# A fused attention and long-convolution kernel: ScalarE instead of GpSimd issues half of four output stores at the end

## The chip, the core and the metric

The kernel runs on one core of a Trainium2 chip. The core has a matrix engine (TensorE, PE in the profile), a vector engine (VectorE, DVE), an engine for activations and copies (ScalarE, ACT), a general engine (GpSimd, POOL) and one that only issues transfers and waits (SyncE, SP). Sixteen DMA engines move data between the core's memory and DRAM; SP, ACT and POOL can issue transfers to them, each through its own queue. Each engine works through its own list of instructions in order. The metric is the device time of one execution in microseconds (us).

## The reference, cut to what matters

Eight batches of 3136 rows. For each batch:

```
scores = z @ z.T / 3136                 # 3136 x 3136, z has 64 columns
attn   = max(scores, 0) ** 2
x      = u * (attn @ v)                 # 3136 x 256
x1, x2, x3 = split(x @ w_proj)          # 3 parts of 256 columns
conv   = irfft(rfft(x2, axis=rows) * rfft(filter, axis=rows))
out    = (x1 * conv * x3) @ w_out       # 3136 x 256, float32
```

The output of one batch is 3136 x 256 numbers of four bytes, 3.2 MB.

## The kernel before, in words

A batch's rows are cut into seven chunks of 512, 512, 512, 512, 512, 256 and 320 columns of the transposed work (`CHUNKS`, line 23), each of two to four tiles of 128 rows. For each chunk the scores are made on TensorE, squared after a relu by ScalarE and VectorE, and multiplied with `v`. The result is multiplied with `u`, projected with `w_proj`, and its middle part goes through a Fourier transform written as matrix products in two stages, with a scratch array in DRAM between the stages. When a batch's spectrum is done, `add_end` (line 1315) finishes it chunk by chunk: it loads the chunk of the convolution (`load_c`), does the last small transform on TensorE (`mm`), multiplies it with the gates on VectorE (`ev`, line 1342), multiplies with `w_out` on TensorE (`mo`), copies the product from the matrix engine's result banks to a tile of the core's memory on ScalarE or VectorE (`eo`, line 1378; such a copy is called an eviction below), and stores the tile (`store`, line 1400).

The order of all instructions is written by a planner when the program is made (`Plan`, line 184). Each piece of work is a `Task` with a cost on one or several engines, the tasks it needs, and the buffers it takes. The planner keeps a clock for each engine, and always emits the task that can start first by those clocks. For ACT, DVE, SP and POOL the method `pick` (line 336) chooses, by the start, then by priority, then by the order in which the tasks were made. A task that moves data has an argument `moves`, and `run` (line 231) adds the delay `DMA_GO` of the issuing engine (line 63), the time on a common bus, and `DMA_DONE`. None of this happens on the chip: there each engine simply runs its list, and waits at semaphores.

The last batch ends differently from the others (line 1865). Its chunks are finished in the order `FINAL`, which is 0, 2, 4, 6, 1, 3, 5, with the flag `split=True`, and their output tiles lie in buffers that are free by then: chunks 0 and 6 in `R_t`, chunks 2, 1 and 5 in `xh`, chunks 4 and 3 in `gs_t`. These names show which chunk a line of the profile belongs to. With `split`, a chunk's tile of 128 partitions is stored in two halves of 64 partitions:

```
elif split:
    s_ = on("POOL", lambda nt=nt, store=store: store(0, nt, (0,), nc.gpsimd), 0.6, [*oe, *behind], moves=0.22 * nt)
    s_ = on("SP", lambda nt=nt, store=store: store(0, nt, (1,)), 0.8, [*oe, *behind], prio=1, moves=0.22 * nt)
```

So POOL issues half 0 of chunks 0, 2, 4, 6, 1 and 3, and SP half 1. Both wait for all evictions of the chunk (`oe`). The last chunk, 5, has a branch of its own (lines 1406 to 1412): one task of SP, in which SP issues half 0 and ACT half 1. A half is 256 KB, that of chunk 6 on POOL 192 KB, and the halves of chunk 5 and the second of chunk 6 are 128 KB.

After the program's last instruction of each engine stands a closing part, which the profile puts down to line 1932: every engine drains, SP waits for the last transfers, and POOL leads a barrier of all engines.

Of the kernel before, what the change touches and what calls it, by code (L numbers as in the profile page):

```python
# [59 lines left out]
    return sum(n / 2400 + 0.003 for n in ns)  # L60


DMA_GO, DMA_DONE = {"SP": 0.3, "POOL": 2.0}, 0.9
LAT = {"PE": 0.22, "ACT": 0.22, "DVE": 0.19, "POOL": 0.15, "SP": 0.0}


# [327 lines left out]
def kernel(  # L394
# [10 lines left out]
    nc = tc.nc  # L405
# [136 lines left out]
    def job(kind, emit, cost, deps=(), takes=(), **kw):  # L542
        if not isinstance(cost, dict):
            cost = {"PE": cost}
        return plan.add(Task(emit, cost, deps, takes, **kw), kind)
# [4 lines left out]
    def on(engine, emit, cost, deps=(), takes=(), **kw):  # L550
        return job(None, lambda e: emit(), {engine: cost}, deps, takes, **kw)
# [18 lines left out]
    def rows_n1(x):  # L570
        return x.rearrange("(n1 n2) d -> n1 n2 d", n2=N2)

    def runs(lo, hi):
        got = []
        for c in range(NC):
            a, b = max(lo, T0[c]), min(hi, T0[c + 1])
            if a < b:
                got.append((0, a, b, NT - T0[c + 1] + a - T0[c]))
        if lo < min(hi, NT - 1):
            got.append((1, lo, min(hi, NT - 1), NT + lo))  # L580
        return got
# [138 lines left out]
    for i, (t0, t1) in enumerate(zip(z_cuts, z_cuts[1:])):  # L720
        step_ = -(-(t1 - t0) // -(-(t1 - t0) // 8))
        for g0 in range(t0, t1, step_):
            nt = min(step_, t1 - g0)
# [375 lines left out]
    for t0 in range(0, NT, 2):  # L1099
        nt = min(2, NT - t0)  # L1100
# [214 lines left out]
    def add_end(b, lasts, gtasks, cs, kind="FB", src=c_p, dsts=(o_p,), late=0, behind=(), then=(), split=False, mids=(y_p,)):  # L1315
        for at, c in enumerate(cs):
            t0, nt = T0[c], len(tiles[c])
# [42 lines left out]
            oe = []  # L1360
# [39 lines left out]
            def store(i0, n, only=(0, 1), by=nc.sync, c=c, ob=ob):  # L1400
                r = rows_n1(out[b])
                for j, lo, hi, n2 in runs(T0[c] + i0, T0[c] + i0 + n):
                    if j in only:
                        by.dma_start(out=r[:, n2 : n2 + hi - lo, :], in_=ob["o"][ds(j * N1, N1), i0 : i0 + hi - lo, :])

            if split and c == cs[-1]:

                def both_queues(nt=nt, store=store):
                    store(0, nt, (0,))
                    store(0, nt, (1,), nc.scalar)  # L1410

                s_ = on("SP", both_queues, 0.6, [*oe, *behind], prio=1, moves=0.45 * nt)
            elif b == B - 2:
                s_ = on(
                    "POOL", lambda nt=nt, store=store: store(0, nt, by=nc.gpsimd), 1.2, [*oe, *behind],
                    moves=0.45 * nt, late=LATE_POOL,
                )
            elif split:
                s_ = on("POOL", lambda nt=nt, store=store: store(0, nt, (0,), nc.gpsimd), 0.6, [*oe, *behind], moves=0.22 * nt)
                s_ = on("SP", lambda nt=nt, store=store: store(0, nt, (1,)), 0.8, [*oe, *behind], prio=1, moves=0.22 * nt)  # L1420
            else:
                s_ = on("SP", lambda nt=nt, store=store: store(0, nt), 1.3, [*oe, *behind], prio=1, moves=0.45 * nt, late=LATE_OUT * (dst is o_p))
# [333 lines left out]
    for gi, g in enumerate(groups):  # L1756
        deps = []
        for un in g:
            b, c, k = un
# [20 lines left out]
        for i, un in enumerate(g):  # L1780
            b, c, k = un
# [46 lines left out]
            if last:  # L1828
# [24 lines left out]
                if c == NC - 1:  # L1853
                    mine = [x for x in x_evs if x[0] == b]
                    gts = [t for x in mine for t in x[2]]
                    lasts = add_spectrum(b, [p for x in mine for p in x[1]])
                    last_spec = loads[-1:]
                    if b < B - 2:
                        add_end(b, lasts, gts, range(NC))
                    elif b == B - 2:  # L1860
                        add_end(b, lasts, gts, range(HOLD))
                        held = lasts, gts
                        held_w = w_
                    else:
                        add_end(b, lasts, gts, FINAL, "FB", A_p, (R_p, xh_p, gs_p, R_p, xh_p, gs_p, xh_p), split=True, mids=(y_p, uT_p))
                        early = [*held[0], held_w]
                        outs = (cut_out, cut_out, cut_out, o_p)
                        add_end(b - 1, early, held[1], range(HOLD, NC), "FZ", cut_in, outs, 4, [(last_spec[0], ISSUED)], [q_])
                        for t in put_back:
                            join(t, inverses[-1], ISSUED)  # L1870
                        late_ones = plan.queues["FZ"]
                        waiting = [t for t in late_ones if t.left and any(d in inverses for d, _ in t.deps)]
                        kids = [k for t in waiting for k in t.kids if k.kind == "FZ"]
                        rest = [t for t in late_ones if t not in waiting and t not in kids]
                        plan.queues["FZ"] = rest + [t for t in late_ones if t in waiting or t in kids]
                    if b == 0:
                        hold = Held(v_p.slots, v_slot[0])
                        w_.frees.append((hold, 0))
                    else:
                        w_.frees.append((cv[b][0], 0))  # L1880
# [56 lines left out]
```

## Time and profile before

| | |
|---|---|
| time, median of 3 runs | 990.45 us (990.18 to 990.82) |
| the profiled execution | 992.91 us, of which the span from first to last instruction is 991.0 us |
| busy over the span | PE 95%, ACT 87%, DVE 84%, POOL 21% |
| granted TensorE clock, mean | 0.989 |
| last instruction that computes | ends at about 979.85 us of the span |
| last issue of a store | starts at 980.83 us of the span |

Times inside the profile are counted from the span's start. A row of the timeline shows the start, the length, the engine, the line of the program, the operation and the tile; a "q" behind the engine (SPq, ACTq, POOLq) marks an instruction of its sequencer: an issue of a transfer, a wait or a drain. The length of an issue is the time for which the issuing engine was held, not that of the transfer. A row of grouped instructions shows the smallest, median and largest length in ns, and the starts of the first and the last. A row of a window shows for a stretch of time the busy time of each engine with the number of instructions, then the granted clock, the busy share of the DMA engines, and what they moved in GB/s. A row of waits shows who waited for whom, with the total, the number and the longest, in us.

### The profile page before, as it was taken

Reading aid. Unit: us, or ns where it says so; the run is one execution under the profiler, and the core shown is the slowest. Engines: PE = TensorE matmul, PEld = TensorE weight load, DVE = VectorE, ACT = ScalarE, POOL = GpSimd, SP = SyncE. Lnnn points to the kernel's source line nnn. Section 1 sums busy time; section 2 is a strip of 40 time slices with the busy share of each in tenths; the row PEclk is TensorE's granted clock in tenths of the full one; section 3 lists DMA queues with packets and bytes.
Section 4 is the critical chain, followed back from the end, with each engine's and each line's share of the span. In section 5 each row is a group of like instructions: output and inputs, shape, how many; then the busy total and the mean of one; then the engine's idle time right before and its main releaser. Section 6 shows DMA issues by size and latency. Waiting matters only on the chain.

```text
span 991.0 us, 19581 instructions
## 1 busy us (share of the span) xinstructions
PE 946.0 (95%) x6774; PEld 471.2 (48%) x6878; DVE 831.3 (84%) x1461; ACT 857.8 (87%) x1192; POOL 207.7 (21%) x430
## 2 busy tenths in 40 slices
PE   6999999999999999999999999999999999999984
PEld 2344544455544545445454444445454455544643
DVE  7966798999798887988789887898879988799874
ACT  5988888899888997899988989799988899998673
POOL 5142311212021312113111320122202230001031
PEclk9999999999999999999999999999999999999978
DMA  9799879979899679997799788997889968985676
GB/s 159 144 174 168 134 151 169 177 131 168 190 206 179 127 150 220 195 174 149 148 219 200 152 137 161 218 200 136 162 171 220 193 126 175 186 219 108 167 214 199
DMA packets 332355, 170.32 MB, mean 172 GB/s; under 512 B 242582, under 2 KB 307926, under 8 KB 332256
## 3 DMA queue, kind: packets, MB, share of 16 engines
q1 hardware_dynamic: 302720, 132.82, 63.3%
q0 software_dynamic: 29456, 36.12, 23.6%
q8 instruction: 54, 0.88, 0.4%
q14 instruction: 45, 0.37, 0.1%
q10 hardware_dynamic: 80, 0.13, 0.0%
HBM read 90.26 MB, written 53.35 MB: 145 GB/s over the span
## 4 chain that ended last, share of the span: by engine, by line
PE 77%; DVE 7%; issue 6%; ACT 4%; DMA 4%; SPq 1%; POOL 1%; POOLq 0%; ACTq 0%; DVEq 0%
PE ps_o_t L523 44%; PE ps_s L523 32%; DVE A_t L1801 4%; ACT R_t L1792 3%; DVE xT_t L1843 1%; DMA uT_t<-un_t 1%; DMA spec<-s_t 1%; DMA ost_t<-in_z_dram 1%; DMA M_t<-spec 1%; ACT s_t L556 1%; SPq L996 0%; DMA specf<-s_t 0%; DVE gs_t L560 0%; ACT gs_t L556 0%; DVE xh L1250 0%
## 5 line engine op out<-in xcount | busy, mean ns | idle before, releaser
L1792 ACT ACTIVATE R_t<-ps_s 128x1024 f32<-128x1024 f32 (+4 forms) x512 | 467.5, 963 | 83.0 <-PE ps_s L523 79.3
L523 PE MATMUL ps_o_t<-A_t,v_t 128*128 128x512 bf16 (+4 forms) x2006 | 447.2, 353 | 11.9 <-issue 5.2
L1801 DVE TENSOR_TENSOR A_t<-R_t 128x1024 bf16<-128x1024 f32 (+2 forms) x324 | 354.1, 1112 | 55.5 <-ACT R_t L1792 55.0
L523 PEld LDWEIGHTS <-v_t 128*128 128x128 bf16 (+1 forms) x2884 | 248.9, 98 | 260.6 <-issue 81.4
L1799 ACT ACTIVATE A_t<-R_t 128x1024 bf16<-128x1024 f32 (+3 forms) x172 | 175.0, 1026 | 1.2
L523 PE MATMUL ps_s<-zT_t 64*64 64x512 bf16 (+4 forms) x1526 | 173.5, 358 | 1.5 <-DVE zT_t L560 0.5
L606 POOL COPY tick<-xT_t 1x1 bf16<-1x1 bf16 x54 | 19.5, 362 | 695.9 <-DVE xT_t L1843 695.9
L523 PE MATMUL ps_s<-xT_t,wp 128*128 128x512 bf16 (+2 forms) x418 | 102.8, 352 | 4.5 <-ACT R_t L1792 2.3
L523 PEld LDWEIGHTS <-zT_t 64*64 64x64 bf16 (+1 forms) x1559 | 52.1, 101 | 107.8 <-issue 93.2
L556 ACT ACTIVATE x_t<-ps_s 128x512 bf16<-128x512 f32 (+2 forms) x170 | 89.7, 583 | 11.8 <-PE ps_s L523 10.1
L1843 DVE SCALAR_TENSOR_TENSOR xT_t<-ps_o_t,uT_t 128x256 bf16<-128x256 f32 (+2 forms) x224 | 76.0, 382 | 8.7 <-PE ps_o_t L523 5.6
L523 PE MATMUL ps_o_t<-M_t,v_t 128*128 128x512 bf16 (+2 forms) x352 | 82.3, 353 | 0.1
L1250 DVE TENSOR_TENSOR xh<-xh,H 128x1024 bf16<-128x1024 bf16 x120 | 82.0, 684 | 0.2
L1162 DVE TENSOR_TENSOR gate_t<-ps_s,x_t 128x256 bf16<-128x256 f32 (+2 forms) x212 | 70.3, 383 | 14.0 <-PE ps_s L523 12.9
L1344 DVE TENSOR_TENSOR yT_t<-ps_s,gate_t 128x512 bf16<-128x512 f32 (+2 forms) x100 | 59.0, 619 | 11.1 <-PE ps_s L523 10.3
L523 PEld LDWEIGHTS <-wp 128*128 128x128 bf16 x448 | 42.9, 98 | 47.1 <-issue 11.0
L597 POOL DMA_DIRECT2D un_t<-in_u_dram x112 | 59.8, 556 | 6.4 <-issue 4.5
L616 POOL DMA_DIRECT2D v_t<-in_v_dram x112 | 59.4, 555 | 3.8 <-PE ps_s L523 1.7
L560 DVE CAST xh<-ps_s 128x512 bf16<-128x512 f32 x61 | 41.1, 688 | 22.6 <-PE ps_s L523 21.3
L523 PE MATMUL ps_s<-wp,xT_t 128*128 128x256 bf16 x396 | 56.3, 273 | 0.1
L523 PE MATMUL ps_s<-wo,yT_t 128*128 128x256 bf16 (+1 forms) x350 | 51.7, 274 | 1.7 <-DVE yT_t L1344 1.7
L556 ACT ACTIVATE s_t<-ps_s 128x512 bf16<-128x512 f32 (+1 forms) x82 | 46.8, 589 | 2.1 <-PE ps_s L523 1.1
(160 smaller groups left out, 828.4 us busy)
## 6 DMA issues: line engine op xcount, KB each, us to landing
out_dram<-ost_t SPq DMA_DIRECT2D x60, 256.0 KB
spec<-s_t SPq DMA_DIRECT2D x96, 128.0 KB
spec_in_t<-spec SPq DMA_DIRECT2D x60, 192.0 KB
spec<-gs_t SPq DMA_DIRECT2D x59, 192.0 KB
v_t<-in_v_dram POOLq DMA_DIRECT2D x80, 128.0 KB, 4.4
un_t<-in_u_dram POOLq DMA_DIRECT2D x80, 128.0 KB, 5.1
conv_in_t<-spec SPq DMA_DIRECT2D x33, 256.0 KB
out_dram<-ost_t SPq DMA_DIRECT2D x18, 128.0 KB
```

The lines of the kernel that those rows point to most:

```text
L523: wrote(nc.tensor.matmul(o, *args, **kw), o)
L556: got = nc.scalar.activation(out_, in_, AF.Copy)
L560: got = nc.vector.tensor_copy(out_, in_)
L597: nc.gpsimd.dma_start(out=t[ds(j * N1, N1), lo - t0 : hi - t0, :], in_=x[:, n2 : n2 + hi - lo, :])
L616: nc.gpsimd.dma_start(out=t[ds(j * N1, N1), ds(v_at(a), (b - a) * D)], in_=r[:, n2 + a - lo : n2 + b - lo, :].rearrange("p t d -> p (t d)"),)
L1162: got = nc.vector.tensor_tensor(g[:, ::-1] if h == 0 else g, p, x, ALU.mult)
L1250: nc.vector.tensor_tensor(x[:, 1 - i], x[:, 0], h, ALU.mult)
L1344: got = nc.vector.tensor_tensor(yb["y"][:, dh, 0:w], p, gates[b, c, dh][:, 0:w], ALU.mult)
L1792: has_read(nc.scalar.activation(blocks(box["R"], n, cw)[:rows], p, AF.Relu), p)
L1799: nc.scalar.activation(a, r, AF.Square)
L1801: nc.vector.tensor_tensor(a, r, r, ALU.mult)
L1843: nc.vector.scalar_tensor_tensor(x, f, inv_s2, ut, ALU.mult, ALU.mult)
```

## The change

For the third to sixth chunk of the last batch's order (4, 6, 1 and 3), half 0 is issued by ACT instead of POOL. Chunks 0 and 2 keep POOL, chunk 5 keeps its branch, and SP's halves stay. The planner is given a delay for transfers that ACT issues, and the cost of such an issue on ACT is put at 0.55 us.

```diff
-DMA_GO, DMA_DONE = {"SP": 0.3, "POOL": 2.0}, 0.9
+DMA_GO, DMA_DONE = {"SP": 0.3, "ACT": 0.5, "POOL": 2.0}, 0.9
...
+            elif split and c in cs[:2]:
+                s_ = on("POOL", lambda nt=nt, store=store: store(0, nt, (0,), nc.gpsimd), 0.6, [*oe, *behind], moves=0.22 * nt)
+                s_ = on("SP", lambda nt=nt, store=store: store(0, nt, (1,)), 0.8, [*oe, *behind], prio=1, moves=0.22 * nt)
             elif split:
-                s_ = on("POOL", lambda nt=nt, store=store: store(0, nt, (0,), nc.gpsimd), 0.6, [*oe, *behind], moves=0.22 * nt)
+                s_ = on("ACT", lambda nt=nt, store=store: store(0, nt, (0,), nc.scalar), 0.55, [*oe, *behind], moves=0.22 * nt)
                 s_ = on("SP", lambda nt=nt, store=store: store(0, nt, (1,)), 0.8, [*oe, *behind], prio=1, moves=0.22 * nt)
```

The store on ACT becomes a task like the evictions: the planner places it in ACT's list between them by its own clocks, at the same priority.

## The prediction

> **What bounds the kernel now.** I began with the page's head and its busy shares.
>
> ```profile
> span 991.0 us, 19581 instructions
> PE 946.0 (95%) x6774; PEld 471.2 (48%) x6878; DVE 831.3 (84%) x1461; ACT 857.8 (87%) x1192; POOL 207.7 (21%) x430
> ```
>
> TensorE bounds the kernel as a whole, and POOL is nearly idle. But these are means over 991 us, and the edit touches only the last 18. So the next view is the busy time of all engines in stretches of that end.
>
> ```profile
> core 0: us, PE busy (x) PEld busy (x) DVE busy (x) ACT busy (x) POOL busy (x), PEclk, DMA share, GB/s
> 974.50:977.00 2.50, 2.50 (x31) 2.06 (x29) 2.48 (x5) 2.00 (x4) 1.05 (x2) 1.00 0.90 236
> 977.00:984.50 7.50, 2.27 (x23) 1.61 (x20) 2.03 (x5) 2.39 (x4) 1.59 (x3) 0.92 0.97 318
> 984.50:987.00 2.50, 0.00 (x0) 0.00 (x0) 0.00 (x0) 0.00 (x0) 0.00 (x0) 0.50 0.21 80
> 987.20:990.20 3.00, 0.00 (x0) 0.00 (x0) 0.00 (x0) 0.00 (x0) 0.00 (x0) 0.50 0.00 0
> ```
>
> Three stages show. Until 977 compute is the limit (PE busy 2.50 of 2.50). From 977 to 984.5 it is the DMA engines (0.97 busy, 318 GB/s): the stores are a backlog, and compute ends inside it. From 987.2 to 990.2 nothing computes and nothing moves (0 GB/s). So what is waited for there? The closing part answers, by its instructions from 981 us on, and by SP's waits.
>
> ```profile
> L1932 SPq EVENT_SEMAPHORE x9: 28/28/28, 985.7 to 987.0; - x9
> L1932 SPq DRAIN x2: 7/10/13, 987.1 to 987.2; - x2
> L1932 POOLq DRAIN x1: 10108/10108/10108, 980.1 to 980.1; - x1
> SPq L1932 <- PEq L1932: 3.7, 2, 3.2
> SPq L1932 <- DMA out_dram<-gs_t: 2.9, 1, 2.9
> SPq L1932 <- DMA out_dram<-xh: 0.9, 1, 0.9
> ```
>
> SP waits for the transfers: the first of its nine waits passes at 985.7, the next is held 0.9 us more by a store of chunk 5, so the last transfer has landed at 986.6. At 987.2 SP is through. Then it waits 3.2 us in the barrier. PE is named there, but PE, like ACT and DVE, has had nothing to do since 980. The late one is POOL: its DRAIN starts at 980.1 and takes 10.108 us, to 990.2. The span ends 0.8 us later (991.0). So POOL's drain sets the end, and 3.0 us behind SP.
>
> What holds the drain? The stores on POOL's and SP's queue, and the one on ACT's:
>
> ```profile
> 974.71 0.52 POOL L1404 DMA_DIRECT2D out_dram<-xh  x1 [0.72 <-ACT xh L556]
> 976.06 0.53 POOL L1404 DMA_DIRECT2D out_dram<-gs_t  x1 [0.83 <-ACT gs_t L556]
> 977.06 0.53 POOL L1404 DMA_DIRECT2D out_dram<-R_t  x1 [0.47 <-ACT R_t L556]
> 978.60 0.53 POOL L1404 DMA_DIRECT2D out_dram<-xh  x1 [1.00 <-ACT xh L556]
> 980.10 0.53 POOL L1404 DMA_DIRECT2D out_dram<-gs_t  x1 [0.98 <-ACT gs_t L556]
> 973.20 0.54 SPq L1404 DMA_DIRECT2D out_dram<-R_t  x1
> 974.44 0.97 SPq L1404 DMA_DIRECT2D out_dram<-xh  x1
> 975.80 0.47 SPq L1404 DMA_DIRECT2D out_dram<-gs_t  x1
> 976.46 1.26 SPq L1404 DMA_DIRECT2D out_dram<-R_t  x1
> 978.33 1.32 SPq L1404 DMA_DIRECT2D out_dram<-xh  x1
> 979.84 0.90 SPq L1404 DMA_DIRECT2D out_dram<-gs_t  x1
> 980.83 1.92 SPq L1404 DMA_DIRECT2D out_dram<-xh  x1
> 979.89 0.55 ACTq L1404 DMA_DIRECT2D out_dram<-xh  x1
> ```
>
> The drain stands right behind POOL's last store (chunk 3, 980.10). Time to landing of that store, and of chunk 2's:
>
> ```profile
> DMA to landing us min/median/max: 5.5/5.5/5.5
> DMA to landing us min/median/max: 4.2/4.2/4.2
> ```
>
> Chunk 3's lands at 985.6, and the drain lasts 4.5 us beyond that. One drain can't tell whether it runs 10.1 us from the last issue or 4.5 us from the last landing.
>
> **The change part by part.**
>
> *POOL's queue loses four stores.* Their 4 x 0.53 us of issue were on no path, since POOL otherwise idled. What counts is the drain: POOL's last store is now chunk 2's, at 974.71, and the drain begins behind it. Counted from the issue it ends at 974.7 + 10.1 = 984.8; counted from the landing at 974.7 + 4.2 + 4.5 = 983.4. Either is before SP's 987.2, so the drain leaves the path and next late is SP. If SP stays where it is, the end is 987.2 + 0.8 = 988.0: 3.0 us less. The bound on the other side is a drain tied to the last landing of any store (986.6, so 3.6 us behind it); it would stay at 990.2 and the gain would be zero. I take the gain, since the drain is POOL's own and has only POOL's list before it.
>
> Here a price of the Trainium skill can be set beside the row of 10.108 us. The page "DMA: Bandwidth & Descriptors", section "Anatomy of one DMA — SWDGE (gpsimd) path", gives about 2.0 us fixed plus bytes / 436e3 for a transfer that POOL issues; an estimate from it for 256 KB is 2.6 us. By it POOL would be done near 983, SP would set the end already, and the sum would be 0 instead of 3.0. The row differs, and decides: the drain takes 10.1 us.
>
> *The planner's list.* Up to chunk 4's evictions no task has changed, so all until 975.8 stays as it was.
>
> *ACT gains four issues.* ACT's evictions from there on, and the two on DVE for chunk 5:
>
> ```profile
> 975.83 0.60 ACT L556 ACTIVATE R_t<-ps_s 128x512 f32<-128x512 f32 x1
> 976.39 0.38 ACT L556 ACTIVATE R_t<-ps_o_t 64x256 f32<-64x256 f32 x1
> 977.05 0.60 ACT L556 ACTIVATE xh<-ps_s 128x512 f32<-128x512 f32 x1 [0.28 <-PE ps_s L523]
> 977.71 0.60 ACT L556 ACTIVATE xh<-ps_o_t 128x512 f32<-128x512 f32 x1
> 978.56 0.60 ACT L556 ACTIVATE gs_t<-ps_o_t 128x512 f32<-128x512 f32 x1 [0.25 <-DMA out_dram<-xh]
> 979.21 0.60 ACT L556 ACTIVATE gs_t<-ps_s 128x512 f32<-128x512 f32 x1
> L560 DVE COPY xh<-ps_s 128x256 f32<-128x256 f32 x2 | 0.8, 424 | 0.7 <-PE ps_s L523 0.7
> ```
>
> From 975.83 to 979.81 they fill about 3.4 of 4.0 us, so 0.6 us are free. Three stores (chunks 4, 6, 1) come ahead of chunk 3's evictions. At best each costs what ACT's own store costs, 0.55: 3 x 0.55 - 0.6 = 1.0 us later. While the DMA engines are full, though, an issue can be held: SP's for the same three chunks took 0.47 + 1.26 + 1.32 = 3.05, which gives 2.4 us. So chunk 3 is evicted 1.0 to 2.4 us later, at 980.8 to 982.2. TensorE waits for those result banks too, and chunk 5 may slip as much. The planner believes 0.55, so it won't move evictions to DVE for more than that.
>
> *What this does to the last landing.* Compute ends inside the backlog, so its delay is mostly cover used up. SP's store of chunk 5 was held at issue to 980.83 + 1.92 = 982.7 anyway. With 318 GB/s, chunks 3 and 5 (512 + 256 KB) are 2.5 us of the DMA engines' work, so everything before them runs to 984.5 - 2.5 = 982. Chunk 3's stores, issued at 980.8 to 982.2, need a little over 1 us to reach the engines, if I take the start of the busy stretch (974.5) behind SP's first store (973.20). So at the early end there's no hole, and at the late end one of 3.4 - 2.0 = 1.4 us. The last landing moves by 0 to 1.4 us.
>
> A gain is possible as well: between 974.5 and 977 only 236 GB/s moved, and stores that no longer pass POOL could fill some of that. Chunk 4's store issues 0.26 us earlier on SP than on POOL (975.80, 976.06), so I bound it at 0.3 us. Between -0.3 and +1.4 I take +0.3: the backlog covers the early end fully, and the only store in ACT's queue shows the cheap price.
>
> *Nothing else.* The bytes and the halves are the same, SP keeps its seven stores, and its waits at the end are as many; I price these at nothing. ACT's closing part lies behind the last eviction and under the transfers.
>
> **Sum.** 991.0 - 3.0 + 0.3 = 988.3 us of span, 2.7 less. The profiled execution took 992.9 in all, so 1.9 lie outside the span, and it is 2.5 over the median of the runs; I carry the difference to the median: 990.45 - 2.7 = 987.75, about 987.8. About 0.2% (2.0 us) is what a measurement of this kernel can tell from no change.
>
> **The rivals.**
>
> 1. *ACT takes POOL's place as the late one, and eats the gain.* Each issue is held like SP's last, 1.92 us. Then 3 x 1.92 - 0.6 = 5.2 us fall before chunk 3's eviction, at 985.0. Landing 4.2 us behind its issue (POOL's second store), it is there at 989.2, 2.6 later than now, and only 0.4 of the gain stay: 990.0. With less holding it lies between 988.5 and this. For it: SP's row of 1.92, and that twice as many stores go by SP's kind of queue. Against it: each queue held only its third and later stores for long (0.54, 0.97 and 0.47 for the first three on SP), and ACT's starts empty.
>
> 2. *The drain does not follow POOL's stores.* If POOL drains 3.6 us behind the last landing of all, the end is 986.6 + 0.3 + 3.6 + 0.8 = 991.3 of span, 990.75 by the median. For it: one drain only. Against it: POOL's DRAIN has no transfer of others in its list. A rule of the Trainium skill speaks on this side: "DMA: Bandwidth & Descriptors", section "Issuing engines are not separate DMA queues", says that all issued transfers end up on the same 16 DMA engines, and that issuing from several saves only issue time, usually small. By it the transfers would end as before, as the row of 318 GB/s makes me expect too, and nothing would be gained; but it doesn't speak of a drain.
>
> 3. *Slower: ACT blocks TensorE.* Issues stand in ACT's list ahead of evictions for which TensorE waits. A hold of 3.0 us each gives 3 x 3.0 - 0.6 = 8.4: chunk 3 at 988.2, landed at 992.4, and with SP's 0.6 and the barrier's 0.8 a span of 993.8, 993.3 by the median. It decides from about 2.7 us an issue on. No row shows a hold that long.
>
> **How the numbers follow.** Forecast 0.70 (987.1 to 988.4), rival 1 0.13 (988.5 to 990.0), rival 2 0.10, rival 3 0.07. Faster by over 0.2% means under 988.47, so the forecast alone: 0.70. Rivals 1 and 2 count as the same: 0.23. Slower 0.07. The range goes from 987.0, a bit under the -0.3 end (990.45 - 3.3 = 987.15), to 990.2, which takes in rival 1 and leaves out rivals 2 and 3; that is a little over 8 in 10.
>
> **What would show it.** POOL's DRAIN starts at 974.7 and ends by about 985. SP's 3.2 us wait in the barrier is gone, and the end follows SP's drain by 0.8 us. ACT's queue has five stores on line 1404, most near 0.55 us, and chunk 3's second `gs_t` eviction ends at 980.8 to 982.2. SP's last waits pass at 986.3 to 988. A drain that still ends near 990 makes rival 2 right; ACT issues of 2 us and more and a last landing behind 988 make rival 1 or 3 right.

## The result and the profile after

The changed kernel takes 988.14 us against 991.26 us of the kernel before, medians of 22 runs each taken side by side. The ratio is 0.9965 with a 95% interval of 0.9952 to 0.9978, so it saves about 3.5 us (2.2 to 4.8); the two medians themselves are 3.1 us apart.

The profiled execution has a span of 985.5 us, 5.5 less than before. Only part of that is the change. SP's first store of the last batch starts at 970.80 instead of 973.20, and up to chunk 4's evictions, which lie behind it, each engine's list is the same in both kernels. These 2.4 us differ from one execution to the next: in another kernel of this study with the same list the same store started at 976.97. So I count the end from that store: 17.76 us before (973.20 to 990.97) and 14.67 after (970.80 to 985.47), 3.1 us less.

The stretches of the end of the changed kernel, with the same columns as those shown of the kernel before. The first three are moved by 2.4 us against them, and the last is what is left of the fourth:

```profile
972.10:974.60 2.50, 2.50 (x31) 2.06 (x29) 2.49 (x5) 1.66 (x3) 0.52 (x1) 1.00 0.87 231
974.60:982.10 7.50, 2.42 (x23) 1.60 (x19) 2.77 (x6) 1.85 (x4) 0.00 (x0) 0.84 0.95 300
982.10:984.60 2.50, 0.00 (x0) 0.00 (x0) 0.00 (x0) 0.00 (x0) 0.00 (x0) 0.50 0.36 136
984.70:985.40 0.70, 0.00 (x0) 0.00 (x0) 0.00 (x0) 0.00 (x0) 0.00 (x0) 0.50 0.00 0
```

The compute stage and the backlog of stores are much as they were (PE busy 2.50 of 2.50 us, then 300 GB/s against 318). What's gone is the stretch of 3 us in which nothing moved; 0.7 us of barrier are left. The closing part, whose line is now 1935, shows why:

```profile
L1935 SPq EVENT_SEMAPHORE x8: 28/28/28, 981.7 to 984.6; - x8
L1935 SPq DRAIN x2: 7/10/13, 984.6 to 984.7; - x2
L1935 POOLq DRAIN x1: 9274/9274/9274, 972.3 to 972.3; - x1
```

POOL's drain now starts at 972.3, behind chunk 2's store, and ends at 981.6. SP is through at 984.7, so POOL has been waiting for 3.1 us when SP comes. SP's own waits, in total, times and longest:

```profile
SPq L1935 <- DMA out_dram<-xh: 2.1, 2, 1.4
SPq L1935 <- DMA out_dram<-gs_t: 1.8, 1, 1.8
SPq L1935 <- PEq L1935: 0.7, 2, 0.5
```

The wait of 3.2 us in the barrier (its row names PE, but POOL was the late one) has become one of 0.5 us. What ends last now is the landing of chunk 3's store (`gs_t`).

The stores in the queues of POOL and ACT, and SP's first one, in the timeline:

```profile
970.80 0.54 SPq L1404 DMA_DIRECT2D out_dram<-R_t  x1
...
971.07 0.52 POOL L1404 DMA_DIRECT2D out_dram<-R_t  x1 [8.23 <-ACT R_t L556]
972.30 0.52 POOL L1404 DMA_DIRECT2D out_dram<-xh  x1 [0.72 <-ACT xh L556]
...
973.49 0.56 ACTq L1404 DMA_DIRECT2D out_dram<-gs_t  x1
974.80 1.63 ACTq L1404 DMA_DIRECT2D out_dram<-R_t  x1
977.11 0.50 ACTq L1404 DMA_DIRECT2D out_dram<-xh  x1
978.39 0.71 ACTq L1404 DMA_DIRECT2D out_dram<-xh  x1
979.20 1.11 ACTq L1404 DMA_DIRECT2D out_dram<-gs_t  x1
```

ACT's issues cost 0.50 to 1.63 us. The evictions around them, from the timelines of ACT, DVE and PE:

```profile
974.65 0.60 ACT L556 ACTIVATE xh<-ps_s 128x512 f32<-128x512 f32 x1 [0.62 <-PE ps_s L523]
976.48 0.60 ACT L556 ACTIVATE xh<-ps_s 128x512 f32<-128x512 f32 x1 [1.24 <-PE ps_s L523]
977.71 0.66 ACT L556 ACTIVATE xh<-ps_s 128x256 f32<-128x256 f32 x2 [0.63 <-ACT xh L556]
...
974.32 0.41 DVE L560 COPY R_t<-ps_o_t 64x256 f32<-64x256 f32 x1
976.25 0.69 DVE L560 COPY gs_t<-ps_o_t 128x512 f32<-128x512 f32 x1 [0.27 <-PE ps_o_t L523]
977.83 0.69 DVE L560 COPY gs_t<-ps_s 128x512 f32<-128x512 f32 x1 [0.89 <-PE ps_s L523]
...
974.67 0.60 PE L523 MATMUL ps_s<-wo,yT_t 128*128 128x256 bf16 x4
977.13 0.60 PE L523 MATMUL ps_s<-wo,uT_t 128*128 128x256 bf16 x4 [0.70 <-ACT xh L556]
```

Chunk 1's two evictions on ACT (`xh`, 512 wide) stand 1.83 us apart instead of 0.66, because ACT was held by chunk 6's store between them: the product for the second one was done on TensorE at 975.27, ACT was held until 976.43, and took it up at 976.48. TensorE then waited 0.70 us for the bank. The planner moved chunk 6's second eviction and both of chunk 3 to DVE and chunk 5's two to ACT, and stored chunk 5 ahead of chunk 3. The last eviction ends 7.72 us behind SP's first store, 1.1 later than before (6.65).

### The profile page after: what moved, and what is told of

Same layout as the page of the kernel before. It is cut to its first block, busy times and chain, and to the rows that moved or that the text cites. A ratio compares the mean times of both kernels' runs of the same rounds, so it can differ in the third digit from the quotient of the medians.

```text
span 985.5 us, 19582 instructions
## 1 busy us (share of the span) xinstructions
PE 944.9 (96%) x6774; PEld 470.5 (48%) x6878; DVE 832.2 (84%) x1462; ACT 856.5 (87%) x1191; POOL 205.6 (21%) x426
## 4 chain that ended last, share of the span: by engine, by line
PE 79%; DVE 8%; ACT 4%; issue 4%; DMA 3%; SPq 1%; POOL 0%; ACTq 0%; DVEq 0%; POOLq 0%
PE ps_o_t L523 45%; PE ps_s L523 33%; DVE A_t L1804 5%; ACT R_t L1795 3%; DVE xT_t L1846 1%; DMA spec<-s_t 1%; DMA ost_t<-in_z_dram 1%; DMA M_t<-spec 1%; ACT s_t L556 1%; DVE gs_t L560 1%; DVE gate_t L1162 0%; DVE xh L1250 0%; DMA specf<-s_t 0%; SPq L996 0%; ACT gs_t L556 0%
```

## The experiments

The theory: POOL's drain set the end, and it follows POOL's own last store, so any way of taking late stores off POOL saves the same. The main rival: the gain comes from ACT's queue, whose transfers start earlier or run better beside SP's. A second question is whether ACT's holds cost something. All kernels were timed beside the kernel before.

**One: SP instead of ACT.** SP issues both halves of chunks 4, 6, 1 and 3; ACT and DVE have the lists of the kernel before.

```diff
             elif split:
-                s_ = on("ACT", lambda nt=nt, store=store: store(0, nt, (0,), nc.scalar), 0.55, [*oe, *behind], moves=0.22 * nt)
-                s_ = on("SP", lambda nt=nt, store=store: store(0, nt, (1,)), 0.8, [*oe, *behind], prio=1, moves=0.22 * nt)
+                s_ = on("SP", lambda nt=nt, store=store: store(0, nt), 1.3, [*oe, *behind], prio=1, moves=0.45 * nt)
```

> SP issues both halves of chunks 4, 6, 1 and 3; ACT's list and DVE's list are those of the kernel before. Theory (POOL's drain set the end, who issues instead hardly matters): POOL's last store is chunk 2's, its drain ends some 3 us ahead of SP's, the gain is that of the change, 3.0 to 3.5 us, ratio 0.9965 to 0.997, less up to 1 us where SP's doubled issues are held. Rival (the gain comes from ACT's own queue, whose transfers start beside SP's): no gain, ratio 0.999 to 1.002, since all eight halves stand in one queue.

The ratio is 0.9954 (0.9937 to 0.9970), and the end lies 14.46 us behind SP's first store. The drain of POOL:

```profile
L1934 POOLq DRAIN x1: 9274/9274/9274, 973.7 to 973.7; - x1
```

It ends at 982.9, ahead of SP at 985.9. ACT's queue isn't needed for the gain; the rival, which asked for 0.999 to 1.002, falls.

**Two: the changed kernel with a small late store on POOL.** POOL issues 16 of the 64 partitions of chunk 3's half 0, 64 KB, and ACT the other 48.

```diff
+            elif split and c == cs[-2]:
+                s_ = on("POOL", lambda nt=nt, store=store: store(0, nt, (0,), nc.gpsimd, p1=16), 0.6, [*oe, *behind], moves=0.06 * nt)
+                s_ = on("ACT", lambda nt=nt, store=store: store(0, nt, (0,), nc.scalar, p0=16), 0.55, [*oe, *behind], moves=0.16 * nt)
+                s_ = on("SP", lambda nt=nt, store=store: store(0, nt, (1,)), 0.8, [*oe, *behind], prio=1, moves=0.22 * nt)
```

> As the changed kernel, but POOL issues 16 of the 64 partitions (64 KB) of chunk 3's half 0, its last store again, and ACT the other 48. All other lists are the same. Theory, counted from the landing: the drain ends 4.5 to 4.8 us behind that small store's landing (some 3 to 4.5 us behind its issue), so 7.5 to 9.3 us behind the issue. Counted from the issue: 9.3 to 10.1 us. Either way POOL is late again, and 1 to 3 us of the gain are lost: ratio 0.998 to 1.000. Rival (the gain is in earlier transfers): ratio stays at 0.9965.

The ratio is 0.9998 (0.9983 to 1.0013): one small transfer on POOL gives the whole gain back. The drain, and SP's wait in the barrier:

```profile
L1939 POOLq DRAIN x1: 9339/9339/9339, 984.3 to 984.3; - x1
```

```profile
SPq L1939 <- PEq L1939: 3.1, 2, 2.6
```

The drain takes 9.3 us, although the store is a quarter as large and lands 4.2 us behind its issue. So it isn't the size of POOL's last store that counts, and SP again waits 2.6 us for POOL (the row names PE, which had nothing left to do).

**Three: only chunk 3 goes to ACT.** POOL keeps chunks 0, 2, 4, 6 and 1, and all evictions stand as before.

```diff
-            elif split and c in cs[:2]:
+            elif split and c in cs[:5]:
```

> Only chunk 3's half 0 goes to ACT, behind all of ACT's evictions; evictions and DVE's list are those of the kernel before. POOL's last store is chunk 1's. Theory: POOL still ends last, but its last issue is 1.5 us earlier and its last landing 1.4 us earlier, so the span is 1.4 to 1.5 us shorter than before: ratio 0.9985. Rival (any store off POOL helps by earlier transfers): a quarter of the gain, 0.8 us, ratio 0.9992.

The ratio is 0.9982 (0.9968 to 0.9995), some 1.8 us. That interval takes in the rival's 0.9992 as well, so here the profile decides: the end is at 15.74 us, 2.0 earlier than before. The drain and the landing of POOL's last store:

```profile
L1935 POOLq DRAIN x1: 9591/9591/9591, 977.6 to 977.6; - x1
DMA to landing us min/median/max: 5.1/5.1/5.1
```

POOL is still last, and its drain begins 1.5 us earlier against SP's first store (5.4 instead of 6.9) and is 0.5 us shorter. That is the 2.0; the theory had put 1.4 to 1.5 on it, from the earlier start alone.

**Four: POOL stores nothing of the last batch.** ACT issues half 0 of all six chunks.

```diff
-            elif split and c in cs[:2]:
+            elif split and c in cs[:0]:
```

> POOL issues none of the last batch's stores; ACT issues half 0 of all six chunks. POOL's last transfers are small stores of the batch before, some 9 us earlier, that land within 2.7 us. Drain counted from the landing: 7.2 to 7.5 us long; from the issue: 9.3 to 10.1 us. It was off the path already, so no further gain by the drain; two more issues on ACT ahead of evictions cost 0 to 1.5 us against the change: ratio 0.9965 to 0.998.

POOL's last two stores are now those of the batch before, ahead of the backlog (the DMA engines were 0.74 to 0.77 busy from 964 to 966 us):

```profile
L1404 POOL DMA_DIRECT2D out_dram<-ost_t x2: 541/551/561, 963.6 to 964.1; - x2
DMA to landing us min/median/max: 2.6/2.6/2.7
```

```profile
L1935 POOLq DRAIN x1: 9227/9227/9227, 964.0 to 964.0; - x1
```

They land within 2.7 us, and still the drain takes 9.2 us. A drain that only runs a fixed 4.5 us beyond the landing is out. The ratio is 0.9943 (0.9926 to 0.9960), and the end is at 13.72 us. I had expected no further gain and 0.9965 to 0.998, so this was a miss; seven and eight take it up again.

**Five: a late landing on POOL.** The kernel before, but POOL stores both halves of chunk 3.

```diff
+            elif split and c == cs[-2]:
+                s_ = on("POOL", lambda nt=nt, store=store: store(0, nt, by=nc.gpsimd), 1.2, [*oe, *behind], moves=0.45 * nt)
             elif split:
```

> The kernel before, but POOL stores both halves of chunk 3 (512 KB, two transfers) and SP none of that chunk. It asks what POOL's drain is counted from where the last landing is late. Theory now (after runs of six kernels): the drain ends at the later of 9.2 us behind POOL's last issue and 4.5 us behind POOL's last landing. The last landing should be 6 to 7 us behind its issue, so the drain ends 10.5 to 11.5 us behind that issue, and the kernel is 0.5 to 2 us slower than before: ratio 1.0005 to 1.002. Rival (a fixed time behind the last issue): 9.2 to 10.1 us, ratio 1.0003 to 1.0008, since the last issue is only some 0.5 us later.

```profile
L1934 POOLq DRAIN x1: 10853/10853/10853, 978.8 to 978.8; - x1
DMA to landing us min/median/max: 5.8/6.0/6.2
```

The last store lands 6.2 us behind its issue, and the drain ends 10.8 us behind that issue, 4.6 behind the landing. A fixed time behind the issue is out as well. In the profile the end is 1.2 us later than before (18.96 us); the ratio, 1.0010 (0.9994 to 1.0026), doesn't tell that from no change.

**Six: no hold on ACT, POOL's drain still hidden.** POOL keeps chunks 0, 2 and 4, SP issues both halves of chunks 6 and 1, and ACT that of chunk 3, behind all evictions.

```diff
-            elif split and c in cs[:2]:
+            elif split and c in cs[:3]:
...
+            elif split and c in cs[3:5]:
+                s_ = on("SP", lambda nt=nt, store=store: store(0, nt), 1.3, [*oe, *behind], prio=1, moves=0.45 * nt)
```

> POOL keeps half 0 of chunks 0, 2 and 4; SP issues both halves of chunks 6 and 1; ACT issues half 0 of chunk 3, behind all its evictions. ACT's and DVE's evictions stand as in the kernel before. Counted from SP's store of chunk 0, POOL's last issue is at 2.9 us and its drain ends at 12.1. Theory (holding ACT ahead of evictions cost the change some of its gain): SP is through at 12.9 to 13.4 instead of 13.9 in the changed kernel, span from that store 13.7 to 14.2, ratio 0.9945 to 0.9958. Rival (the holds cost nothing, only the drain counted): 13.9 and 14.7 as in the changed kernel, ratio 0.9965.

The evictions end early, at 6.66 us, but SP is through only at 14.27 and the end is at 15.03, 0.4 us later than in the changed kernel. The ratio is 0.9977 (0.9967 to 0.9987); the changed kernel, timed with it as seven, has 0.9969 (0.9959 to 0.9980), so the times don't tell the two apart. SP's stores of chunks 6 and 1, two each:

```profile
975.13 2.19 SPq L1404 DMA_DIRECT2D out_dram<-R_t  x2
977.42 2.56 SPq L1404 DMA_DIRECT2D out_dram<-xh  x2
980.07 1.65 SPq L1404 DMA_DIRECT2D out_dram<-gs_t  x1
```

SP is held from 975 to the end of its list. Both expectations missed: without any hold on ACT the tail got longer, not shorter.

**Seven and eight: the changed kernel and the fourth one again, side by side.**

> The changed kernel again, on the chip of the others of this call, as their measure: ratio 0.9965, SP through 13.9 us behind its store of chunk 0, the end at 14.7.

> The kernel in which POOL stores nothing of the last batch, again, beside the changed kernel on one chip. If its lead is real: ratio 0.9935 to 0.9955, SP through 12.9 to 13.2 us behind its store of chunk 0. If it was the chip: as the changed kernel, 0.996 to 0.997 and 13.9 us.

The changed kernel has 0.9969 (0.9959 to 0.9980) and ends at 14.64 us; the other has 0.9962 (0.9950 to 0.9974) and ends at 13.73. In the profiles both repeat to 0.03 us, so the fourth kernel's tail is 0.9 us shorter (SP is through at 12.97 us, as a real lead would have it). In the times the intervals overlap, so a lead over the changed kernel isn't shown there.

**Nine: the tipping point.** POOL keeps chunks 0, 2, 4 and 6.

```diff
-            elif split and c in cs[:2]:
+            elif split and c in cs[:4]:
```

> POOL keeps half 0 of chunks 0, 2, 4 and 6; ACT issues that of 1 and 3. POOL's last issue is 3.9 us behind SP's store of chunk 0. By the rule from the runs so far (the later of 9.1 to 9.4 us behind the issue and 4.4 to 4.6 us behind the landing) the drain ends at 13.0 to 13.4, while SP was through at 12.9 to 14.3: the point where neither leads by much. Theory: the end is at 13.8 to 14.7 behind that store, ratio 0.9945 to 0.997, and SP waits for POOL under 0.5 us. If the drain were a fixed 10.1 us: end at 14.8, ratio 0.997.

```profile
L1935 POOLq DRAIN x1: 9451/9451/9451, 975.5 to 975.5; - x1
DMA to landing us min/median/max: 4.7/4.7/4.7
```

The drain ends 13.29 us behind SP's first store and SP is through at 12.99: POOL is late by 0.3 us. The rule from the earlier kernels, which the first table below shows, had put the drain's end at 13.0 to 13.4 ahead of the run. The end is at 14.07, the ratio 0.9957 (0.9942 to 0.9973).

**Ten: ACT's stores behind its evictions.** The changed kernel with a lower priority for them.

```diff
-                s_ = on("ACT", lambda nt=nt, store=store: store(0, nt, (0,), nc.scalar), 0.55, [*oe, *behind], moves=0.22 * nt)
+                s_ = on("ACT", lambda nt=nt, store=store: store(0, nt, (0,), nc.scalar), 0.55, [*oe, *behind], prio=1, moves=0.22 * nt)
```

> As the changed kernel, but the planner gives ACT's stores a lower priority than evictions, so chunk 6's second eviction stays on ACT and chunk 6's store comes behind both of chunk 1's evictions. If the holds on ACT cost the change something, compute ends earlier (last eviction under 7.7 us behind SP's store of chunk 0) and the end comes before 14.6; if the DMA engines' backlog covers them, the end stays at 14.3 to 14.8 whatever the evictions do. Ratio 0.996 to 0.9975.

```profile
975.44 0.60 ACT L556 ACTIVATE xh<-ps_s 128x512 f32<-128x512 f32 x1 [0.29 <-PE ps_s L523]
976.09 0.60 ACT L556 ACTIVATE xh<-ps_o_t 128x512 f32<-128x512 f32 x1
976.15 0.48 ACTq L1404 DMA_DIRECT2D out_dram<-R_t  x1
976.73 1.28 ACTq L1404 DMA_DIRECT2D out_dram<-xh  x1
```

Chunk 1's evictions are 0.65 us apart again, and the last eviction ends at 7.19 us. The end is at 13.75 us, 0.9 earlier than the changed kernel's, and the ratio is 0.9960 (0.9946 to 0.9974), which the times alone can't tell from 0.9965.

**The two tables behind these readings.** First POOL's drain, in us, from the start of POOL's last issue, worked out from the rows of each profile (the drain's start and length, the issue, the landing):

| kernel | landing | end of the drain | drain beyond the landing |
|---|---|---|---|
| four, batch before | 2.74 | 9.11 | 6.37 |
| two, 64 KB | 4.16 | 9.32 | 5.16 |
| one | 4.39 | 9.25 | 4.86 |
| changed | 4.49 | 9.25 | 4.76 |
| nine | 4.74 | 9.43 | 4.69 |
| six | 4.98 | 9.40 | 4.42 |
| three | 5.07 | 9.57 | 4.50 |
| before | 5.54 | 10.09 | 4.54 |
| five | 6.17 | 10.76 | 4.58 |

All nine fit one rule: the drain ends at the later of 9.1 to 9.4 us behind the last issue and 4.4 to 4.7 us behind the last landing. Nine was forecast from the others; for the rest the rule was drawn from the rows themselves. The rows don't tell its second half from another reading: the drain's end also rises with the number of stores that POOL issued in the last batch (9.11 us with none, 9.25 with two, 9.32 and 9.40 with three, 9.43 with four, 9.57 with five, 10.09 with six, 10.76 with seven), and no kernel had a late landing with few stores on POOL, or an early one with many. What POOL does in that time no row shows.

Second the tail, in us behind SP's first store of the last batch:

| kernel | last eviction | last landing | SP through | POOL's drain ends | end of span |
|---|---|---|---|---|---|
| before | 6.65 | 13.38 | 13.96 | 16.98 | 17.76 |
| changed | 7.72 | 13.50 | 13.90 | 10.76 | 14.67 |
| one, SP both | 6.53 | 13.37 | 13.70 | 10.75 | 14.46 |
| two, small late store | 7.59 | 13.86 | 14.20 | 16.62 | 17.40 |
| three, POOL five | 6.65 | 12.36 | 12.94 | 14.97 | 15.74 |
| four, POOL none | 7.24 | 12.73 | 12.95 | 0.61 | 13.72 |
| five, POOL more | 6.65 | 13.59 | 13.84 | 18.17 | 18.96 |
| six, no hold on ACT | 6.66 | 13.87 | 14.27 | 12.26 | 15.03 |
| nine, POOL four | 6.66 | 12.46 | 12.99 | 13.29 | 14.07 |
| ten, ACT later | 7.19 | 12.60 | 12.99 | 10.76 | 13.75 |

In each row the end is the later of the two columns before it, and 0.8 us. The last landing lies between 12.4 and 13.9 us and doesn't follow the last eviction: evictions that end at 6.66 go with 12.46 and with 13.87.

## Why the prediction was right

*What bounds the end.* Right. The drain behind POOL's last store was the late one, by 3.0 us, and when the store moved, the drain left the path. Experiments one and two show it from both sides.

*Which reading of the drain.* The prediction carried two, 10.1 us from the issue and 4.5 us from the landing. Neither is right alone, as four and five show; for the changed kernel they gave an end of 984.8 or 983.4 on the old clock, and 10.76 us behind SP's first store is 984.0 there. The gain didn't hang on it.

*The term of +0.3 us for a later last landing.* It measured +0.1 (13.38 to 13.50). That needn't mean that the backlog covered the later evictions: with the same bytes the last landing came 0.6 to 1.0 us earlier than before in three, four, nine and ten (12.36 to 12.73), so the 0.3 us that bounded a gain was too small, and the +0.1 may be an earlier finish and a cost of ACT's holds that cancel. No run shows the two apart.

*ACT's evictions.* Chunk 3 was evicted 1.1 us later (7.72 against 6.61), inside the predicted 1.0 to 2.4, but not by the predicted path, so the agreement is luck. The step that failed is that the planner "won't move evictions to DVE for more than that": it moved three there and two to ACT, and turned the order of chunks 5 and 3. It was also wrong that a queue holds only its third and later stores for long: of ACT's five the second was held 1.63 us, the third 0.50, and SP's third before had been held only 0.47. "Most near 0.55" fits three of the five at best (0.56, 0.50, 0.71).

*The sum.* 2.7 us were forecast. The tail of the profile gives 3.1, the times 3.5 (2.2 to 4.8). The difference in the tail: SP was through 0.06 us earlier (13.90 against 13.96) where I had it 0.3 later. The landing slipped by 0.1 only, and SP's waits behind it took 0.40 us instead of 0.58, since more of them had passed already. That the time itself, 988.14 us, lies so close to the forecast 987.75 is partly luck: the kernel before measured 0.8 us more in these runs than the 990.45 that the forecast started from, and the two medians lie 0.4 us further apart than forecast, so two deviations partly cancel.

*The rivals.* Rival 1, ACT as the new late one, didn't come: holds there were, up to 1.63 us, and TensorE waited 0.70 us, but the landing moved by 0.1. Rival 2, a drain that follows the last landing of all stores, falls by one row: the drain ended at 981.6, while chunk 3's store landed at 984.3. The rule beside it, that issuing from several engines saves only issue time, of the Trainium skill's page "DMA: Bandwidth & Descriptors", section "Issuing engines are not separate DMA queues", fits the transfers of three kernels: the last landing is at 13.4 us with POOL or SP issuing the moved stores and at 13.5 with ACT. It doesn't account for kernel three, which moved one store from POOL to ACT, kept every eviction and SP's list, and had its last landing at 12.36; there is one profile of it. The gain of the change lay elsewhere, in a drain of the issuing engine. Rival 3, slower, needed issues of 2.7 us; the longest was 1.63.

*What stays open.* Tails of the same bytes differ by up to 1.5 us in the last landing, the same kernel's repeats by 0.03. Ten suggests that ACT's hold between chunk 1's evictions costs 0.9 us of the tail, and six that keeping ACT free doesn't help when SP has to issue more. Which order and sharing of queues lets the DMA engines finish early wasn't settled. Kernels four, nine and ten have shorter tails than the changed one, by 0.6 to 0.95 us, but in the times none of them is told apart from it.

## What to carry to other kernels

At the end of a kernel, look at which engine's drain ends last, not only at the last transfer: here an engine that was 21% busy and had no work left held the end for 3 us. In this kernel a transfer on POOL's queue stays off the path only if it's issued a good 9 us before the other engines are through; a 64 KB one gave back the gain as a large one does. And price moved issues in the list they move to: ScalarE was held 0.5 to 1.6 us for each, the last eviction came 1.1 us later, and the variant that kept the stores out from between those evictions had a tail 0.9 us shorter.

## What the runs showed of the hardware

- POOL's drain behind a transfer lasts at least 9.1 us from its issue, even where the transfer has landed after 2.7 us, and in the profiles with a landing later than 4.7 us it ended 4.4 to 4.7 us behind that landing (or, what these runs don't tell from it, later with more stores on POOL's queue).
- The first store of the last batch on SP's and on ACT's queue held its engine for 0.54 to 0.57 us in every profile, later ones for 0.47 to 1.92 us on SP and 0.48 to 1.70 us on ACT. What sets the length no row shows.
- The profiled executions reached the first store of the last batch anywhere from 970.8 to 977.0 us, with the same instructions up to there; a tail has to be compared from such a mark, not from the span's start.
